# Splitting the key and query products of a segment in two, in a newly planned order of instructions

## The chip, the core and the metric

The kernel runs on one core of a Trainium2 chip. The metric is device microseconds (us) of one execution; the kernel before took 809.02 us (median of three runs, 808.73 to 811.75). Names of engines: PE multiplies matrices (PEld is its weight load, which overlaps PE), DVE and ACT are the vector and the scalar engine, POOL is GpSimd, SP issues the transfers (DMA).

## What is computed

Two attention layers read the same 2048 x 512 input `x`, and a gate mixes their outputs. Everything is bf16.

```python
g = sigmoid((x * gate_w).sum(-1, keepdims=True))
a = A(x, mem0, Wq, Wk, Wv, Wo)           # 32 heads of 128, 64 segments of 32 tokens
b = B(x, wq, wk, wv, wo, beta)           # 32 heads of 16, 4 stages of 512 tokens
return g * a + (1 - g) * b

# A: a recurrence. Each segment attends over 8 memory rows and its own 32 tokens,
# and the 8 memory rows of its output are the next segment's memory.
for s in range(64):
    h = concat([mem, x[32 * s:32 * s + 32]])                # 40 x 512
    q, k, v = h @ Wq, h @ Wk, h @ Wv                        # 512 -> 32 heads x 128
    p = softmax(mask(q @ k.T / sqrt(128)))
    o = (p @ v) @ Wo                                        # back to 512
    mem, out[s] = o[:8], o[8:]
# B: per stage a causal softmax over 512 tokens, plus a linear-attention memory
# of the stages before, mixed by sigmoid(beta) per head; then @ wo.
```

So A is 64 steps, each of which needs the output product of the one before; B has no such chain, except a small sum from stage to stage.

## The kernel before, in words

**Tiling.** In a segment of A only 32 rows (24 tokens and the 8 memory rows) are multiplied when the segment comes; the other 8 tokens of each segment don't depend on the memory in their projections and are done for four segments at once, ahead of time ("rest" work, `p_rest`: `rq`, `rk`, `rv`). With 32 rows as the stationary side, PE is split into four column tiles of 32, so that four products run side by side: a projection of 512 features onto half of the heads (`r` = 0 or 1) is 4 chunks `c` of the 512 features times 4 tiles, 16 matmuls of 512 columns. `wproj` writes it. A segment `s` (`p_seg`) is, by the names used below:

- `k0`, `q0`, `k1`, `q1`: key and query products of the two halves of the heads (tile `pb<-Wk_sb,hT`, `pb<-Wq_sb,hT`; line 1466 for products with a weight load, line 124 where the weights already in PE are used again). `q1` is done as two pieces of 256 columns. Each is evicted from PSUM (line 1040) and transposed by DVE (line 1544).
- `v0`, `v1`: value products (`pb<-Wv_sb,hT`), each in four pieces of one chunk, with other work allowed between the pieces.
- `H`, `S`: mask and scores (lines 1067 and 1559, 1563); `exp` on ACT (1568).
- `U`: the softmax sums by a product with ones (1586 and 124); ACT makes the reciprocals as exp(-ln) (1589, 1591), DVE multiplies them in (1593; the part of the rest rows in 1595, on DVE or POOL).
- `PV`, `PW`: probabilities times own values and times rest values (1626, 1635), evicted by ACT and DVE (1040).
- `wo`: the output product, 8 pieces of 8 matmuls of 256 columns (1352). DVE transposes the sum (1370), two small copies swap its halves (1374, each on ACT or DVE), and an addition writes the memory columns of the next segment's `hT` (1377). The first projection of the next segment waits for that.

B's work (`b...`: logits `bL` line 1184, their exps 1202, masks on POOL 1208, values `bPV` 1225, projections `bk`, `bq`, `bV`, rows `brow`), the rest work and its output product `wor` are put between the steps of A, to cover A's waits.

**Rest values.** `rv` of four segments is evicted into one of three staging tiles `stg` and stored to DRAM by four transfers (`rvst`, line 1431, `rest_v<-stg`), from where later segments load it (`rem_v<-rest_v`). A staging tile goes around: the next work that is given the tile may not be evicted into it before all four stores have landed, and since PSUM banks of this kind of work are handed out whole, the product itself waits for that too.

**What sets the order.** Every step is recorded with what it reads and writes. The order of instructions on each of the five queues (PE, ACT, DVE, POOL, SP) is fixed: it is unpacked from the table `ORDER`, a packed list of numbers, made by a planner of which the class `Prog` has the constants. Some steps may go to one of two engines; which one is in the table too. The planner's model of time (costs of steps; `FETCH`, the least time from one packet of 256 PE instructions to the next; `load`, the time that a store occupies the path to memory) puts out no instruction. It set the order, and with the table given it still decides which of the eight PSUM banks a step gets, and which semaphore a step has to look at.

**Weights kept.** `Share` and `turn`: where two projections of a segment stand directly behind each other on PE, the second starts with the chunk whose 32 columns of `hT` are still loaded, and leaves that weight load out (line 124).

```python
            for _ in range(o.size):
                c = held[1] if held and held[0] == key and held[1] in left else left[0]
                o.plan.append((c, held != (key, c), len(left) == o.share.total, len(left) == 1))
```

Of the kernel before, what the change touches and what calls it, by code (L numbers as in the profile page):

```python
# [15 lines left out]
    "c-nPY2Vhji)1STeF4uA?v>=^?&|5%yhY+L$k)VQrAcWpkgiu0n(u)*9k<bOC_Z~XZi6|=kK|vr1sdu@%x9^*MS6(^31g`Acot^TV-^^~-M`r8XMp|Ig6oFooTVNYGXX@;)^wVtFn%O{L-i3n@*B#C`"  # L16
    "cT8)`LDw(V+82JAtt+I@qaW7dJ+F6O<rWX!RP=Jz<srAqWx$1DtA>?2_3if0W`@qlw5DbQY`7VjYwVpKQ)%I}LVoT<LJ8;GqD_E^HxQonL(&U?D!)}Z7!SLWTI$>Y`$7ugVO=9QjPTkF@LQGo06jhD"
    "&Q3Ym!9(@~!1dJ0nwXEtthlv}Yv|lJp+VC#zq_F3L-=~*fA|>6Xh}2vQj3=*&viP~>T>O<pIcsQ05@`Mjp1%BfO83ln}0VFZl8rF=_!Q(99wdt9qcs~m_GUek_jPtx7o=#PoGH*b!d1EK+VT#Jz+=6"
    "%sy=PxfW~ztO2<4e)@5K?MQRBz1}H(c-0FQPazm_`ZIvaZa6aHwO=~g1P1FTL~G41=E~KYxJ&@EM+^5M&JDi;v?>5FdM6%*0+YQXuhp6z#<%u@Fjt-^a>GbBoc<ba0T{gV;LDw;Qpx5QU*TNdhC4y1"
    "tN9t6+H`(9H^jj_NR+m(p7wC5XFWhSo^uo5WIzSpz<bY1Km~Xnm<eTI;m)h59<L{8*i#(Hw_;S>`2btSFG@zwCG>thRTBM2_dVVBKy!Za1VSu0Y}Pq7kUQ!7{E_IQ<T({3)0(B=%euRwzF$s<5H2gE"  # L20
    "&;*OdgUJosf1fFt)((cPy4vtD3Cqztv=-g<xE!1dM(s6-Go5V$%bQ+=asK_MrlQ99Q|U3TCwg0ck=0pf*Fi3v=n;LlCcr%={xrl(;&%_hIKs`BBuxKW@7AFjXA<3c7Wlo~6M!0Sn9ss+O|lT-7XvrU"
    "e-kaQMGKq215}3K15@$}82&mE)=J*{14=b4Lj3$wt<YNRaadM}1_hgpo1i;bVACg(5~~;DO9hW3kDyqa1I+oMPQ-Q>OCId&3C@gIC@u#@e*Fs(Q+Ykw##Df$W7(XDOtfvSy^kcee!poeC-QpqvC#pG"
    "rs^C}xCmf=E}Owg)2jZ-c7KUbCzf@+0qoAgABO<$y%NT-c^q^&hBF?;K*`GMT0M@-vY8z?)$yR(vl`jYAR54}Gr+BSTVgYkVa;c#=$au+ZaIJ)Tj@+uf#$bd1WgFN6H^aiTkDU?4*^wyul>%NG#kD#"
    "o^1)R6Ya{zIOm`q4#&}MnmV_bU58-xF-haQ%`UV!2OXKlm>JW)h7d!xiD_)`>We=u&qA?R#Ts10k5<$mG|wwC8}sKkh(U?Fa>p)C4#Wy|g_wRD`YvYLipb3mojvZ`3Fy?RFd1USXa@FQ3k|Mq7#P=`"
    "C6M0u!7ki66oC%y(&znh78YIm_lg99Ut#hr_!v<@Y*Fw}6uf?8%{3K_TbpNb+4Egy*m{1egsu-^?!?cd+v^>AKC?;@v^&{$U%1=Tb{}HlTHZr+95}`fhL#c-j$s<)W$Yw`<8o}dwgRv>ypV6yusoWs"
    "`w}+&H$~EVJUHN|f!h#b=#94f?L`G)PLgNIv+?Fa-T<!TCGei4O5C=U(6CK|<88FzZyBZ3x?^`%hTFAYq8njv5^RS_|AWsq`^}6MU+oT}%`tOtN;}YTI`^kPYGDQ2*$wOTqb1pxRF#~w`G_3m>w_PF"
    "(Glttb7*a%9llSL(ZsRqaR8aq_=vnsy^FoJ^Lp;(xx`FU0Yo~?9w;<GKBF(6jR!gd4BrSkcPXt^^U{oT@mEQtplrsj%Nn<E!vZ)6kT6NkZ$7p#xg#?5T5$e2f)uVB6uMv}d0u)+3IkM{;Zwg0A5?=?"
# [126 lines left out]
class Slot(Res):  # L154
# [27 lines left out]
class Prog:  # L182
# [17 lines left out]
    FETCH = 3.55  # L200
# [1496 lines left out]
```

## Time and profile before

| | |
|---|---|
| runs | 808.73, 809.02, 811.75 us; median 809.02 |
| the profiled execution | 809.81 us, of which the span of instructions is 808.1 us |
| clock granted to PE | 1.000 over the span |
| PE busy | 788.1 us (98%), 23542 matmuls; 21898 weight loads |
| DVE, ACT, POOL busy | 609.9 us (75%), 560.4 us (69%), 249.1 us (31%) |
| moved by DMA | 45.02 MB, of it 2.92 MB in 178 packets of instructions on one queue |

Rows of the profile give an engine, a line, the tiles (out<-in), the sizes and a count; a row of waits names who waited, for whom, the sum in us, how often, and the longest. Rows of the timeline start with the start in us and the length; what stands in brackets is how long the engine had been idle and what ended it. Four matmuls on four column tiles run at the same time, so a row of four of 512 columns, with 0.39 us, is not four times 0.39. PE counts as busy while any is under way.

### The profile page before, as it was taken

The numbers are of one execution on the slowest core, as the hardware profiler recorded it, in microseconds if no ns is written. First come the engines' busy times: TensorE is split into PE (matmuls) and PEld (weight loads), VectorE is DVE, ScalarE is ACT, GpSimd is POOL, SyncE is SP. The second block draws the span as 40 slices with busy tenths as digits, with TensorE's granted clock in tenths as the row PEclk, the third lists the DMA queues.
The fourth block names the chain that finished last, engine by engine and source line by source line (L and its number), as shares of the span: only waits on it lengthen the run. The fifth ranks groups of instructions, "written<-read, shape, count | busy, mean of one in ns | idle before, by whom it ended". The sixth has DMA issues, their size and how long they took to land.

```text
span 808.1 us, 50000 instructions
## 1 busy us (share of the span) xinstructions
PE 788.1 (98%) x23542; PEld 466.1 (58%) x21898; DVE 609.9 (75%) x1578; ACT 560.4 (69%) x1322; POOL 249.1 (31%) x543
## 2 busy tenths in 40 slices
PE   9989999999999999999999999999999999999997
PEld 4445656656565566555567565565655655556655
DVE  4868776878888777777666777788867788776876
ACT  3676676676766766767777687676677776767773
POOL 3533231232332323431323331433323313323340
PEclk9999999999999999999999999999999999999999
DMA  8992112211111210111011211111020100000011
GB/s 314 417 273 45 44 30 50 44 30 30 46 31 28 41 34 20 45 35 46 20 35 40 46 44 17 33 29 26 28 59 23 43 24 16 11 26 16 17 35 36
DMA packets 71689, 45.02 MB, mean 56 GB/s; under 512 B 50046, under 2 KB 69942, under 8 KB 69942
## 3 DMA queue, kind: packets, MB, share of 16 engines
q1 hardware_dynamic: 70422, 40.92, 18.1%
q8 instruction: 178, 2.92, 1.5%
q10 hardware_dynamic: 1056, 0.92, 0.4%
q14 instruction: 33, 0.27, 0.1%
HBM read 30.33 MB, written 8.87 MB: 49 GB/s over the span
## 4 chain that ended last, share of the span: by engine, by line
PE 88%; DVE 5%; ACT 3%; DMA 1%; issue 1%; POOL 1%; SPq 0%; DVEq 0%; POOLq 0%
PE pb L1466 42%; PE pb L1352 18%; PE pb L124 6%; PE pb L1067 6%; PE pb L1184 4%; PE pb L1069 3%; PE pb L1225 2%; PE pb L1626 2%; PE pb L1559 1%; DMA rest_v<-stg 1%; PE pb L1586 1%; PE pb L827 1%; PE pb L1635 1%; PE pb L1563 1%; PE pb L1273 1%
## 5 line engine op out<-in xcount | busy, mean ns | idle before, releaser
L1040 ACT ACTIVATE st<-pb 128x512 bf16<-128x512 f32 (+2 forms) x291 | 135.3, 489 | 78.7 <-PE pb L1466 68.6
L1202 ACT ACTIVATE PTB<-pb 128x640 bf16<-128x640 f32 x240 | 157.6, 706 | 27.2 <-PE pb L1184 25.1
L1466 PE MATMUL pb<-Wv_sb,hT 128*32 128x512 bf16 x1760 | 139.0, 380 | 0.0
L1352 PE MATMUL pb<-Wo_sb,OT_sb 128*32 128x256 bf16 x4096 | 134.2, 274 | 3.1 <-issue 1.9
L1466 PE MATMUL pb<-Wq_sb,hT 128*32 128x256 bf16 (+1 forms) x2604 | 129.8, 311 | 1.0 <-DVE hT L1377 0.6
L1466 PE MATMUL pb<-Wk_sb,hT 128*32 128x512 bf16 x1716 | 116.5, 379 | 0.2
L1352 PEld LDWEIGHTS pb<-Wo_sb,OT_sb 128*32 128x32 bf16 x4096 | 99.4, 96 | 19.5 <-ACT OT_sb L1040 2.8
L1208 POOL TENSOR_SCALAR_AFFINE_SELECT PTB<-PTB 128x512 bf16<-128x512 bf16 x120 | 78.0, 650 | 98.2 <-ACT PTB L1202 92.8
L1466 PEld LDWEIGHTS pb<-Wq_sb,hT 128*32 128x32 bf16 x2604 | 67.5, 97 | 58.1 <-issue 32.4
L1040 ACT ACTIVATE OT_sb<-pb 128x320 bf16<-128x320 f32 (+2 forms) x162 | 65.7, 426 | 46.2 <-PE pb L1635 45.5
L1466 PEld LDWEIGHTS pb<-Wk_sb,hT 128*32 128x32 bf16 x1716 | 45.8, 97 | 53.3 <-issue 17.5
L1544 DVE STREAM_TRANSPOSE QT_sb<-st 128x128 f32<-128x128 f32 (+1 forms) x192 | 62.5, 336 | 17.3 <-ACT st L1040 15.3
L1595 POOL TENSOR_TENSOR PT_sb<-PT_sb,rc_sb 128x64 bf16<-128x64 bf16 x68 | 25.8, 379 | 155.3 <-ACT rc_sb L1591 154.1
L1544 DVE STREAM_TRANSPOSE KT_sb<-st 128x256 f32<-128x256 f32 x128 | 55.3, 432 | 18.2 <-ACT st L1040 16.5
L1040 DVE CAST V_sb<-pb 128x512 bf16<-128x512 f32 x82 | 56.1, 685 | 14.9 <-PE pb L1466 14.0
L1589 ACT ACTIVATE rc_sb<-pb 128x160 f32<-128x160 f32 x128 | 38.8, 303 | 36.3 <-PE pb L124 36.0
L1370 DVE STREAM_TRANSPOSE pb<-pb 128x256 f32<-128x256 f32 x63 | 29.3, 465 | 44.8 <-PE pb L1352 44.4
L1040 DVE CAST OT_sb<-pb 128x320 bf16<-128x320 f32 x98 | 47.1, 481 | 19.2 <-PE pb L1635 18.3
L1466 PEld LDWEIGHTS pb<-Wv_sb,hT 128*32 128x32 bf16 x1760 | 43.6, 98 | 24.4 <-issue 4.3
L1517 POOL COPY QT_sb<-rem_q 128x256 bf16<-128x256 bf16 x64 | 28.9, 452 | 89.9 <-PE pb L1563 63.0
L1593 DVE TENSOR_TENSOR PT_sb<-PT_sb,rc_sb 128x160 bf16<-128x160 bf16 x128 | 43.8, 342 | 14.4 <-ACT rc_sb L1591 13.1
L1568 ACT ACTIVATE PT_sb<-pb 128x224 bf16<-128x224 f32 x128 | 45.3, 355 | 12.4 <-PE pb L1563 7.9
(211 smaller groups left out, 1576.6 us busy)
## 6 DMA issues: line engine op xcount, KB each, us to landing
Wv_sb<-in_A_Wv_dram SPq DMA_DIRECT2D x4, 1024.0 KB, 10.9
Wk_sb<-in_A_Wk_dram SPq DMA_DIRECT2D x4, 1024.0 KB, 20.3
Wq_sb<-in_A_Wq_dram SPq DMA_DIRECT2D x4, 1024.0 KB, 27.5
Wo_sb<-in_A_Wo_dram SPq DMA_DIRECT2D x4, 1024.0 KB, 21.1
rest_v<-stg SPq DMA_DIRECT2D x112, 32.0 KB
rem_v<-rest_v SPq DMA_DIRECT2D x28, 128.0 KB, 2.3
a_rows<-ao SPq DMA_DIRECT2D x63, 32.0 KB
stg<-a_rows SPq DMA_DIRECT2D x15, 128.0 KB
```

The lines of the kernel that those rows point to most:

```text
L124: return pe.add_instruction(mybir.InstMatmult(name=pe.bass.get_next_instruction_name(), start_tensor_calc=start, stop_tensor_calc=stop, in ...
L1040: self.P.op(("act", "dve"), (lambda a: a.activation(dst, src(), ACT.Copy), lambda d: d.tensor_copy(dst, src())), reads=reads, writes=write ...
L1067: ins = pe.matmul(out[32 * c:32 * c + 32], lhsT[:, 32 * c:32 * c + 32], rhs, start=start, stop=stop, tile_position=(0, 32 * c), **kw)
L1184: ins = pe.matmul(pb[slot.banks[i]][:, base + a - lo:base + b - lo], KT[r0:r1, 128 * kc:128 * kc + 128], Q[r0:r1, t0 + a:t0 + b], start=Tr ...
L1202: P.op("act", (lambda dst=dst, src=src: lambda a: a.activation(dst, src(), ACT.Exp, scale=0.25))(), reads=[pair], writes=["%s%d_%d" % (nam ...
L1208: P.op("gp", (lambda pt=pt, ii=ii: (lambda g: g.affine_select(pt, pt, ([[0, len(ii)]] if len(ii) > 1 else []) + [[1, 128]], ALU.is_ge, 0.0 ...
L1352: ins = pe.matmul(pb[so.b][p0:p0 + 32, 0:256], tok(r, g, l), half(h, d, q), start=(r == 0 and g == 0 and l < 2), stop=(r == 1 and g == 3 a ...
L1466: ins = pe.matmul(out, own, part[:, g], start=start, stop=stop, tile_position=(0, 32 * g))
L1544: op("dve", (lambda dst=dst, src=src: lambda d: d.transpose(dst, src))(), reads=["st%d%s" % (i, tag)], writes=["%sT%d%s" % (kind, r, tag)] ...
L1568: op("act", lambda a: a.activation(PT[:, r, :], pb[rb.b][:, 0:224], ACT.Exp, scale=SCALE), reads=[rb], writes=["PT%d" % r, "PT%dr" % r], n ...
L1589: op("act", lambda a: a.activation(rc[:, r, :], pb[rb.b][:, 0:160], ACT.Ln), reads=[rb], writes=[rr], name="ln%d_%d" % (s, r), cost=0.325, ...
L1593: op("dve", lambda d: d.tensor_tensor(mine[r], mine[r], by_head(rc[:, r, :]), ALU.mult), reads=[rp, rr], writes=[rp], name="nrm%d_%d" % (s ...
```

## The change

Four edits. The key and query products of segments 1 to 63 are recorded as two steps of two chunks instead of one of four (`n` from 1 to 2), so that other PE work can stand between the halves, and either half can begin with the chunk that is loaded; `q1`, already two pieces by columns, becomes four steps. Two of the planner's constants change: `FETCH` from 3.55 to 3.95, and the `load` of each of the four stores of rest values from 0.1 to 0.35. And `ORDER` is another table (three lines longer, so that line 1466 before is line 1469 now, and so on), made with these.

```diff
 ORDER = (
-    "c-nPY2Vhji)1STeF4uA?v>=^?&|5%yhY+L$k)VQrAcWpkgiu0n(u)*9k<bOC_Z~XZi6|=kK|vr1sdu@%x9^*MS6(^31g`Acot^TV-^^~-M`r8XMp|Ig6oFooTVNYGXX@;)^wVtFn%O{L-i3n@*B#C`"
+    "c-nPY2VfM{*8XO;mt@oEAwdvB=p|HXN{3Jtq&)-_LJ8Fe0s=}$Q3N4Cq)3x49qCB#JOrf|6%YYKLJGS{cK6PIW@dM1W;cHzyV*OpobsLToOAbPIIk-({aY+6{G~158R^c87&7w<&#cd96!QFZaF{y*"
 ...
     BLOCK = 256
     BLOCK_AT = 190.0
-    FETCH = 3.55
+    FETCH = 3.95
 ...
                     P.dma(group, lambda s, l=l: s.dma_start(dst[:, :, l, r, :], st[:, 128 * l:128 * l + 128]), reads=[rs], writes=["dv%d_%d_%d" % (j, r, l)],
-                          name="rvst%d_%d_%d" % (j, r, l), prio=prio + 0.001 * l, load=0.1, cost=0.4)
+                          name="rvst%d_%d_%d" % (j, r, l), prio=prio + 0.001 * l, load=0.35, cost=0.4)
 ...
                 self.wproj(rb, kind, r, hv, [rx, rm], "%s%d_%d%s" % (kind, s, r, tag), prio, 4 if kind == "v" or s == 0 else 1,
+                self.wproj(rb, kind, r, hv, [rx, rm], "%s%d_%d%s" % (kind, s, r, tag), prio, 4 if kind == "v" or s == 0 else 2,
                            ("own", s) if s else None, lo, hi)
```

What the new table does on the queues is seen at three places. In the rows of the order, a line, the operation, out<-in, the size of the output, and how many of them follow each other.

**Transfers around the stores of rest values `rv8_0`** (SP). `rest_v<-stg` are the stores of the staging tile, `a_rows<-ao` are rows of finished segments, `DMA_TRANSPOSE xT` fetches input of a later stage. Before:

```order
L1316 DMA stg<-a_rows 128x512
L1487 DMA rem_v<-rest_v 128x512
L1431 DMA rest_v<-stg 4x32x128 x3
L947 DMA_TRANSPOSE xT<-in_A_x_dram 128x4x128
L1662 DMA a_rows<-ao 2x32x256 x2
L1431 DMA rest_v<-stg 4x32x128
L1329 DMA out_dram<-stg 128x512
```

and now:

```order
L1319 DMA stg<-a_rows 128x512
L950 DMA_TRANSPOSE xT<-in_A_x_dram 128x4x128
L1026 DMA wvB_sb<-in_B_wv_dram 128x4x128
L1026 DMA wqB_sb<-in_B_wq_dram 128x4x128
L1434 DMA rest_v<-stg 4x32x128 x3
L1665 DMA a_rows<-ao 2x32x256
L1434 DMA rest_v<-stg 4x32x128
L1332 DMA out_dram<-stg 128x512
```

The fourth store stood behind three other transfers, one of them a transposing one; now it stands behind one.

**From the output product of segment 52 to the first projection of segment 53** (PE). Before:

```order
L1352 MATMUL pb<-Wo_sb,OT_sb 32x256 x56
L1067 MATMUL pb<-hide_sb,neg_sb 32x4x40 x4
L1466 MATMUL pb<-Wk_sb,xr 32x512 x4
L1184 MATMUL pb<-QTm,KT_1 128x320 x4
L1466 MATMUL pb<-Wk_sb,xr 32x512 x4
L1466 MATMUL pb<-Wq_sb,hT 32x512 x16
```

and now:

```order
L1355 MATMUL pb<-Wo_sb,OT_sb 32x256 x64
L1187 MATMUL pb<-QTm,KT_1 128x320 x4
L1469 MATMUL pb<-Wk_sb,hT 32x512 x8
L127 MATMUL pb<-Wq_sb,hT 32x512 x4
L1469 MATMUL pb<-Wq_sb,hT 32x512 x12
```

Four groups of other work stood between the two; now one does, the piece of B's logits. Here the first half of the key product (8 matmuls) is followed by the whole query product, which begins with the loaded chunk.

**From the sums of segment 42 to its probabilities times values** (PE; the first row is the last product with ones, `Wv_sb,hT` are value products of the segment). Before:

```order
L124 MATMUL pb<-PT_sb,ones_sb 32x4x16 x4
L1466 MATMUL pb<-Wv_sb,hT 32x512 x12
L1626 MATMUL pb<-PT_sb,V_sb 128x40 x16
L1635 MATMUL pb<-PT_sb,rem_v 128x4x16 x4
L1184 MATMUL pb<-QTm,KT_1 128x64 x4
L1184 MATMUL pb<-QTm,KT_1 128x256 x4
L1626 MATMUL pb<-PT_sb,V_sb 128x40 x16
```

and now:

```order
L127 MATMUL pb<-PT_sb,ones_sb 32x4x16 x4
L1469 MATMUL pb<-Wv_sb,hT 32x512 x4
L1629 MATMUL pb<-PT_sb,V_sb 128x40 x16
L1638 MATMUL pb<-PT_sb,rem_v 128x4x16 x4
L1187 MATMUL pb<-QTm,KT_1 128x64 x4
L1187 MATMUL pb<-QTm,KT_1 128x256 x4
L1629 MATMUL pb<-PT_sb,V_sb 128x40 x16
```

Eight of the twelve value products have been moved to earlier places of the segment.

Counted over the whole program: 23551 matmuls (23542 before) and 21642 weight loads (21898 before); the weights in PE are used again in 350 groups of four matmuls (283 before). PE changes from one tiling of its array to another 390 times in both. Of the 320 split products, 199 have both halves directly behind each other. 367 transfers on SP in both. DVE has 24 steps fewer (1554 for 1578), ACT 13 more, POOL 11 more.

More of the change, by code (lines that the diff above doesn't have):

```diff
@@ L20 @@
[L20 to L27, printed above, removed]
@@ new lines @@
+    "?Ot5M%u|hV*wlGvzswbb+|hZjpH$RcuU`1?mJ9gdwJvqV!<qS}vqQ3OpBk2ynRYZGJbU<z`C}X(ef>$|z+o}&K4;#l0DSrR<cVOMDSy4LT}+l6i2An2KS09mguU|)W9$1|bDd{br(G~#X#|%UE&#7e"
+    "U+M#NXY6<@Z-M?mtIaoRqstClf-woWc4qU53#g^LSqOclTg9J$Hj`GA)p1SWhUw_LPh!Jzj-b`aT4f)dX?dp6c{Fuh$ckuk<s!yq151W38HG!pHh2w~aiC4Zv%nTwKX853-v)bhraT7<-4<tfMs&uB"
+    "V@vezT)SJped@H{D`wxq>gu=q0Vc>lgOFW+9@_1~qS4UXbM2X}uD&RhLA&a5-S%7uvP!$LyKaIru%huu7*olzdXLrglIOy5^mte+>tP~C&y3(nkXDjV($5~ew#GLGSM0@<8O5?tz(r&o?5(HmEzaa)"
+    "uqFLs#KEbzl+EAh37l!P*D2aSmk*2C<?41qp9!0%`AHma=SI@Z&t`U4=HENF1iY7Vt9oSOU>lN(<Kc0T?Kh_6ivn5W?xTFBPo7O5kb!|Jzl$HOPMGt-Wk!a(%=$a!b-I^UT{gm&1F3GTemzk+qs}gL"
@@ new lines @@
+    "--0B3F$txgi$}ojoG{0(&wowkf^{@77vrauRFvLJziAIh1wE$Df;|&P>+8r&SiL+JjIz!ehjr)HE8D-1?jN`M74DK*QBU+%<k^hbUjBA9$I1He+^h=gAvD8M;8f#O#c5>``<UKrc_x(JUM&hvj`#A-"
+    "&YEkI^&JVgDyjaTmAH;NqEqCbjUxuo>n>4#7u-=fuxFG&HVO6^6?C|TT5imz2~*d+A2{gUxW9ndtDff`m<q||Ufy0CCqZk>(h=ilViM4~ks?`(HE`5ydcsQDlXX!d`*saO{57jF6LwqP0Xn`@dlW~O"
+    "B2{_m)#d?jLO$<}%8JQ;TID59G&S@4(9X7{3tU!&A&($~pSsc1fA_UNKU2g9O((nNn_6vkyowYt0=NEb3pW-Y{zb9w#^K*iB|p5TUp*oVIoc;;%xvd$U{Q`Jgh`Ralz0=U@Z6*G=m|u6*!AD{pxOCO"
+    "8`8(*rDM1_+4QW0JiBC7&kyzP*Y)W1E<G%NWY=>QczFXHSAa^QZLZgMW1DEc{)#a1Kz4YArzE@;wk&#k9uHGK8eP>_xy%FA@4Yz^gRziij-@rTC(5hlU}tBiWdmZK+VX6oQ62hhSWM&te&ffvB!0K?"
@@ new lines @@
+    "XsoDlA4!+cRKltFZ~9!202X7G74}?NVZX0ps{Tf=4hg8@R2xOl@3DB4K;E+1&sWCQ-q_$Bu9m;@4NTkIf0oapB{E<)yb^7+a7@nf$$9fJ9+kwXRHRvqmN<kj%RI$^AM;Ee9bd4gU-D*Jk|iOi)oC{t"
+    "Ui|C25<It&vJ72C6Gc5GYUdp`8qCQf%vqc%>kNgq0uHXtBPHTX-XpGPi{&2=PHGG{0l@VtTK6nE@@_>Zl7U05PS7gr4J1mcU&g{+5|9qH64!l6arEf;V^TaOL(+eJKbZ8n7N=u=sy+9+5ox3GeeN_x"
+    "`w3!L_x}myZ=-Yu!ZXMKaW9>s1<hHaE;hy$z}q|jm`uu(X3^NEBN0v}p+I;pQB%S{M;nkI=#0Is?YWUaM%6nQ!Y@~xQppz&E}My>n<oy0>0v2b-iCd<^ZDf;!@3s##`Hj1)Qe9PD|bTg{CQ+ElFKcz"
+    "_)dyMMCQN7==3ncIXP10_r1u9z$aucatJK>{G0!{$~|+I`(x#p{GDB3ce@ZZWgG;+031yAEwUO4ff~<g|1TG0@Q8dGol)|+@llPJpcVQhz?k`|=q$6J@1VH9;!x&^7+K(6m&hUhuxEkS!&tB~)oUcK"
@@ new lines @@
+    "`IJOE-vq1o@0U#WsI0hZa}v%qXia<|rWo)xNG8tbYT=6H#WsK9sp6Cd`0qRr*BS~9dWu|QSRs+W$&}AiHk~zTf(-c1!#nu2xR<i5R2{g@E^|5HVL^0;K^OIsc+}?6k^kKIrAuJzMX4nvetKY&$mV4j"
+    "^kF$V^!{09a#))m!vDri>7+n+21wmA&!y?cJkfF42zN$gZSN(*WBJH)7lvYb+x;^Xzonw~eXJ9G7WI;gdg;i<)bHf%Xd|IC!Mbz)Ml_K)fPz)0GiT8QM<Gb=oxR)`0=Rxstn%LFug2lcdtv5W(cW%k"
+    "qL|$oMr5CVx3o;e$=Hq3?<gx)i`lzxoE!|aBqGa51ej@d-LCN~u~rj%t_iLoAK(L-i4UMPE%=!@k-V&j!&M;ivCb2vKl(0SiTU9;MqRg3sO)<&>$&LNvM;1_iUS44vScGOoO%Ov))ys~d^Cna#ccfU"
+    "(&n!&EvNA{{njAYK3qjq<mYn~tl>nz#GDd!W|pxyje6vojoUig@|G7Ehf?-37K~Sn`#HW_aDS6jsUYSh(HkZDwVjE1$k}V~AL~ES_!qd+L0PeHGWlk5a=Mg^-1INX8CK=2yaI{%!;K1L43tt_ULP2o"
@@ new lines @@
+    "Zhp#}^LP=g1izf9Y+5kzM;%pwk#4N%9H$sLZRxi60KxNIqFm824j;J10OM(e2?JGJux}($MxEb4ykaruMCOR3PofkU3nJXu*uJc)4*C`wZDz+SCueqXu(<V<R;(UVdcQUOsl;3FMjB4<Q^amT6{;kK"
+    "6=IRaWtd$txv=T(#NDzuE8FrORKnUsG*m2e?EUW}fIbqmMcFA;<iQWXY?N@5DLcOVoy>gAj*Dd?mA}AUaW?ObdHMD9Z0MvFUYnEPP2fg^B2bToSie;wVU<-@4J7U&*ww}pMbnri`JYPZhmwzF`kXAW"
+    "{-j;IY<q7z+0czPIInCw9b$_6NkTPMNSqkJ<Q+MF-B>z7**5|!dRi?3$HWw1RGJ$`4*`uRj7)6~xTW?)&#bfM#X3Q*2Je-YsMeQY?Nrap^DOimCH_$_1NVyK8A=!~S2J8DELTMoach>Sq-d*-r;}*1"
+    "ZxuzAXuY_f;9z;IHRB@C`rzh{j9W*wl6P?D?fUm};r*Vy#gf+|j&ZSL8JkNxm3Zd;#C^Kqd66~TwQj|-EGjpedNvIBn^n#^$2wyVYxzI+4(VnF$L!n8$)!Cudq!+lgzHXSxK|J1(DhKydgo3r!04!~"
@@ L75 @@
+    "3`OP"
 )
```

91 lines of the change are left out of this document (40 added, 51 removed).

## The prediction

> **What bounds the kernel now.** I read the page first: how full PE is, and what the chain that ended last is made of.
>
> ```profile
> span 808.1 us, 50000 instructions
> PE 788.1 (98%) x23542; PEld 466.1 (58%) x21898; DVE 609.9 (75%) x1578; ACT 560.4 (69%) x1322; POOL 249.1 (31%) x543
> ...
> PE 88%; DVE 5%; ACT 3%; DMA 1%; issue 1%; POOL 1%; SPq 0%; DVEq 0%; POOLq 0%
> ```
>
> PE is the bound from end to end, and the change leaves its products as they are. So the only thing to be won or lost is the time in which PE stands still, and the view by stretches says where that is:
>
> ```profile
> 0.00:60.00 60.00, 55.56 (x986) 27.29 (x978) 38.18 (x101) 34.32 (x69) 26.45 (x72) 1.00 0.95 338
> ...
> 60.00:760.00 700.00, 690.75 (x21248) 413.42 (x19704) 536.35 (x1389) 499.51 (x1184) 209.92 (x447) 1.00 0.14 33
> ...
> 760.00:808.00 48.00, 41.78 (x1320) 25.41 (x1216) 35.36 (x90) 26.53 (x72) 12.76 (x26) 1.00 0.11 31
> ```
>
> The first column behind the length is PE's busy time: 4.4 us idle at the start, 9.3 us in the 700 us of steady work, 6.2 us at the end, at a granted clock of 1.00. Some 20 us in all is what an order can touch; 0.5% of the time, about what a measurement of this kernel can tell from no change, is 4.0 us of it. The waits of PE and of its weight load say on whom:
>
> ```profile
> PE pb L1352 <- issue: 2.3, 3, 1.4
> PE pb L1466 <- DMA rest_v<-stg: 1.3, 2, 0.9
> ...
> PE pb L1067 <- issue: 1.0, 3, 0.4
> ```
>
> ```profile
> PEld pb L1466 <- issue: 57.0, 179, 0.8
> ...
> PEld pb L1626 <- DVE PT_sb L1593: 10.0, 28, 0.7
> ...
> PEld pb L1466 <- DVE hT L1377: 6.7, 22, 0.6
> ```
>
> (Us in total, times, longest.) The 57.0 us is no loss: the weight loader idles while PE streams. What counts is the hand-over of the memory (`hT`), the probabilities (`PT_sb`), one store, and a few pauses with no releaser (`issue`).
>
> **The change, part by part.**
>
> *Halves.* The same 16 matmuls per product. Four side by side follow each other at 0.22 and 0.21 us, whether with a weight load or, as in the second row, without:
>
> ```profile
> 375.26 0.39 PE L1466 MATMUL pb<-Wv_sb,hT 128*32 128x512 bf16 x4
> ...
> 375.48 0.39 PE L124 MATMUL pb<-Wv_sb,hT 128*32 128x512 bf16 x4
> ...
> 375.69 0.39 PE L1466 MATMUL pb<-Wv_sb,hT 128*32 128x512 bf16 x4
> ```
>
> One load has this row on the page (mean 97 ns behind the busy time):
>
> ```profile
> L1466 PEld LDWEIGHTS pb<-Wq_sb,hT 128*32 128x32 bf16 x2604 | 67.5, 97 | 58.1 <-issue 32.4
> ```
>
> So the 256 weight loads that are left out (64 groups of four) save nothing on PE: cost 0, hidden under the streaming of the group before; if that cover were gone, 256 x 0.097 us / 4 side by side = 6 us would be at stake. The other bound is a penalty at the new seams; the value products, in single chunks already, show none (0.22, 0.21). Changes of tiling are 390 in both orders. I take 0.
>
> *The store.* The fourth store of `rv8_0`:
>
> ```profile
> 375.46 0.53 SPq L1431 DMA_DIRECT2D rest_v<-stg  x1
> ...
> 376.94 0.40 PE L124 MATMUL pb<-Wv_sb,hT 128*32 128x512 bf16 x4
> ...
> 378.22 0.40 PE L1466 MATMUL pb<-Wk_sb,xr 128*32 128x512 bf16 x4 [0.89 <-DMA rest_v<-stg]
> ```
>
> The value product issued at 376.94 needs 0.22 us; PE could go on at 377.16 and goes on at 378.22, 2.76 us after the store's issue: 1.06 us lost. Now one transfer instead of three stands between the third and fourth store, and the transposing one has been moved ahead of all four. Bounds: 0 (the transfers ahead of the four hold them all back) to -1.06; with 6.3 us of PE work between `rv8_0` and `rk8_0` (6.5 before) and the short queue, I take -1.06. The trace names no other late store, and the other covers are 5 us and up (4.6 us sufficed before). The Trainium skill ("DMA: Bandwidth & Descriptors", on where the 2 us go) puts a store's fixed cost at about 2 us, most of it the write receipt; by that PE would have lost about 0.3 us here, and the term would be -0.3.
>
> *Longer spacing of instruction packets.* The constant issues nothing. What it is meant for looks like this (weight loads in the middle of one run of products, which no other engine releases):
>
> ```profile
> 253.58 0.12 PEld L1352 LDWEIGHTS pb<-Wo_sb,OTr_sb 128*32 128x32 bf16 x7 [0.64 <-issue]
> ...
> 394.44 0.83 PE L1352 MATMUL pb<-Wo_sb,OT_sb 128*32 128x256 bf16 x22 [0.51 <-issue]
> ```
>
> I gave each group on PE its spacing from the rows and cut the order at every 256 PE instructions. Packets that hold under 3.95 us of work: 69 before, 62 now; under 3.55 us: 26 and 31. So the new order isn't thinner where it was dense. Bounds: -3.3 us (the 2.3 and 1.0 of PE's waits for issue all gone) to +3.3; I take 0, as the counts point both ways. The Trainium skill ("Runtime: NRT & Kernel Launch", on instruction fetch) says that crossing a block of 256 instructions is mostly hidden, which would make this term 0 whatever the order; the two pauses above speak against "hidden".
>
> *The new order.* Here is the hand-over from segment 52 to 53 before:
>
> ```profile
> 678.49 0.24 PE L1067 MATMUL pb<-hide_sb,neg_sb 128*32 128x160 bf16 x4
> ...
> 678.56 0.39 PE L1466 MATMUL pb<-Wk_sb,xr 128*32 128x512 bf16 x4
> ...
> 678.72 0.47 DVE L1370 STREAM_TRANSPOSE pb<-pb 128x256 f32<-128x256 f32 x1 [0.26 <-PE pb L1352]
> 679.00 0.10 PEld L1184 LDWEIGHTS pb<-QTm,KT 32*128 32x128 bf16 x4 [0.41 <-ACT PTB L1202]
> 679.01 0.31 PE L1184 MATMUL pb<-QTm,KT 32*128 32x320 bf16 x4
> 679.22 0.19 ACT L1374 ACTIVATE other_sb<-pb 64x32 f32<-64x32 f32 x1 [0.26 <-DVE pb L1370]
> ...
> 679.25 0.40 PE L1466 MATMUL pb<-Wk_sb,xr 128*32 128x512 bf16 x4
> 679.51 0.19 DVE L1377 TENSOR_TENSOR hT<-pb,other_sb 128x32 bf16<-128x32 f32 x1
> 679.75 0.55 PEld L1466 LDWEIGHTS pb<-Wq_sb,hT 128*32 128x32 bf16 x16 [0.40 <-DVE hT L1377]
> 679.76 1.05 PE L1466 MATMUL pb<-Wq_sb,hT 128*32 128x512 bf16 x16
> ```
>
> Transposition, two copies side by side and the addition need 1.27 us from the first matmul after the output product (678.49) to the first projection (679.76). PE's work in it was 0.07 + 0.22 + 0.24 + 0.22 and 0.11 at the change of tiling, 0.86: 0.4 us short. Now only the logits are left, 0.35 us: 0.9 us short. Done so for the hand-overs of segments 3 to 62 (0.16 us more where both copies are on one engine), the work falls short by 3.8 us in 20 of them before and by 5.3 us in 22 now: +1.5 us. Nothing stands in PE's queue that could fill it, so I take it whole.
>
> The same tally for the two other chains. From the sums to the probabilities times values, whose links are
>
> ```profile
> L1040 ACT ACTIVATE OT_sb<-pb 128x320 bf16<-128x320 f32 (+2 forms) x162 | 65.7, 426 | 46.2 <-PE pb L1635 45.5
> ...
> L1589 ACT ACTIVATE rc_sb<-pb 128x160 f32<-128x160 f32 x128 | 38.8, 303 | 36.3 <-PE pb L124 36.0
> ...
> L1593 DVE TENSOR_TENSOR PT_sb<-PT_sb,rc_sb 128x160 bf16<-128x160 bf16 x128 | 43.8, 342 | 14.4 <-ACT rc_sb L1591 13.1
> ```
>
> (two ACT steps of 0.3, one of DVE of 0.34, and the hops: 1.5 us), the shortfall goes from 2.95 to 4.05 us, in segment 42 because 8 matmuls, 0.43 us, left it. From there to the output product (an eviction of 0.43 and 0.3 of hops, as between the output product and its transposition) it goes from 1.75 to 3.3. Together +2.65. These waits take each other's place, as segment 61 shows, where the tally before has 0.9 us in front of the second `PV` and 0.54 in front of `wo`:
>
> ```profile
> 776.54 0.27 PE L1626 MATMUL pb<-PT_sb,V_sb 32*128 32x40 bf16 x16
> ...
> 777.25 1.17 PE L1352 MATMUL pb<-Wo_sb,OT_sb 128*32 128x256 bf16 x36 [0.34 <-DVE OT_sb L1040]
> ```
>
> The trace has 0 and 0.34. Bounds 0 and +2.65; I take half, +1.3. In front of the scores the tally goes from 4.8 to 8.25 in cases of some 0.15 us each, near its resolution, so I take 0 and keep +3.45 as an upper end. DVE gives 24 steps to ACT and POOL, which are at 69% and 31%, so I count nothing for it.
>
> *Sum.* -1.06 + 1.5 + 1.3 = +1.7 us on the profiled 809.8 us: 811.5. That execution lies 0.8 us over the median of the runs (809.0), so 810.7.
>
> **Rivals.**
> 1. *The thinner covers add up.* The mechanism is the wait between engines that the halving and the other order left with less work in it; it decides once half of the tally comes true beyond my sum. For it: every chain's shortfall grew. Against it: segment 61. With all of it, -1.06 + 1.5 + 2.65 + 3.45 = +6.5: 815.5 us, slower.
> 2. *The pauses of issue go.* The planner, told of a longer spacing, left little cover where it expected a pause, so waits and pauses fall together, and covers cost nothing: -1.06 - 3.3 = -4.4: 804.6 us, faster. For it: pauses such as that at 394.44 stood by themselves. Against it: the counts of dense packets. By the skill's page on the runtime this rival has nothing to win; as two rows show such pauses, I leave it its chance.
> 3. *It does nothing.* 199 of 320 pairs of halves stand directly together, the end of the kernel has nearly the same order, and PE's work is the same: 809.0 us, or 808.0 with the store.
>
> **How the numbers follow.** My forecast (0.40) and rival 3 (0.12) lie within 0.5% of 809.0 (805.0 to 813.1) but for a little on each side; rival 1 has 0.23, rival 2 0.25, a little more than the counts of packets give it, since the tally sees only what shrinks on PE's side. Faster 0.26, same 0.49, slower 0.25. As cases of both signs hold half the chance, the likeliest one's own range is 808 to 814. The range for all reaches to rival 2 with 3 us of PE's other idle time gone (801.6), and to rival 1 with a further 2.5 us of the 3.3 of pauses (818.0).
>
> **What would show it.** Right: PE's busy time in the middle still 98 to 99%; the row of `rest_v<-stg` gone from PE's waits; weight loads 21642, with more than 57 us of `issue` on the loader and no time for it; the waits for `hT` L1377 above 6.7 us and for `PT_sb` L1593 above 10.0. Wrong: PE's waits for issue at zero (rival 2), or waits in front of the scores, L1559, grown by more than 2 us (rival 1); a store or a load of rest values late at another segment; a queue on ACT or POOL, with their added steps, that holds up the exps; or a start, before 60 us, that ends at another time, which I took as equal because its transfers bound it.

## The result and the profile after

The changed kernel took 816.13 us (median of 6 runs, 813.7 to 816.81) beside 809.13 us before; ratio 1.0073, 95% interval 1.0053 to 1.0094: slower by 0.7%, some 6 us. I had put 810.7 us and "no change" first; what came is the time of rival 1. It lies outside the 808 to 814 us that I gave my own case, and inside the range for all cases. The profiled execution took 816.68 us. Its page:

```profile
span 814.9 us, 49775 instructions
PE 791.4 (97%) x23551; PEld 453.3 (56%) x21642; DVE 597.8 (73%) x1554; ACT 566.9 (70%) x1335; POOL 254.7 (31%) x554
...
PE 88%; DVE 5%; DMA 3%; ACT 2%; issue 1%; SPq 0%; POOL 0%; DVEq 0%; ACTq 0%; POOLq 0%
```

PE is the bound as before, and DMA has gone from 1% to 3% of the chain that ended last. By stretches (length, then PE's busy time):

```profile
0.00:60.00 60.00, 54.76 (x987) 26.80 (x975) 40.25 (x105) 34.26 (x66) 28.45 (x76) 1.00 0.95 335
60.00:760.00 700.00, 688.22 (x21065) 398.25 (x19289) 517.13 (x1351) 501.44 (x1187) 210.11 (x446) 1.00 0.15 33
760.00:815.00 55.00, 48.38 (x1512) 28.26 (x1384) 40.38 (x99) 31.24 (x82) 16.13 (x34) 0.99 0.11 31
```

PE stands still 5.2 us at the start (4.4 before) and 11.8 us in the 700 us of steady work (9.3 before), and the work left for the third stretch is 6.6 us more. The waits of PE itself, then of its weight load:

```profile
PE pb L1355 <- issue: 2.2, 4, 1.3
PE pb L1469 <- issue: 1.8, 2, 1.4
PE pb L1469 <- DVE hT L1380: 1.6, 5, 0.5
...
PE pb L1469 <- DMA rest_v<-stg: 1.0, 2, 0.8
...
PE pb L1469 <- DMA out_dram<-stg: 0.4, 1, 0.4
```

```profile
PEld pb L1469 <- issue: 69.1, 211, 1.7
...
PEld pb L1469 <- DVE hT L1380: 11.1, 32, 0.7
...
PEld pb L1629 <- DVE PT_sb L1596: 9.4, 26, 0.7
...
PEld pb L1355 <- ACT OT_sb L1043: 5.1, 13, 0.7
...
PEld pb L1355 <- DVE OT_sb L1043: 3.7, 11, 0.6
```

Before, the two rows of `OT` in front of the output product read

```profile
PEld pb L1352 <- ACT OT_sb L1040: 2.8, 8, 0.6
...
PEld pb L1352 <- DVE OT_sb L1040: 2.4, 9, 0.5
```

So `hT` stands at 11.1 us (6.7 before), `OT` at 8.8 (5.2), and the wait for a store of rest values is still there. These rows overlap with work of PE. So I took PE's lost time from the trace: for every two pieces of work that follow each other, the time from the first matmul to the next piece's, less the streaming time and less the median for that pair of kinds. Gaps above 0.06 us go to the operation that ended last before them; where all had long ended they are pauses without a releaser. In us, behind 55 us, one profiled execution each:

| execution | `hT` | `PT` | `OT` | other engines | stores, output | pauses | sum |
|---|---|---|---|---|---|---|---|
| before | 1.9 | 2.4 | 3.8 | 6.5 | 1.1 | 4.1 | 19.7 |
| after | 3.9 | 3.7 | 5.8 | 4.5 | 1.6 | 7.3 | 26.8 |

The sum is 7.1 us up, and the profiled executions are 6.9 us apart. So there are two candidates: the three hand-overs (+5.3, of which 2.0 come back at other engines) and the pauses (+3.2). The limit of 55 us flatters the kernel before, though. The 7.3 us after hold a pause of 1.6 us at 58 us; the 4.1 us before leave out its twin, which starts at 54 us and is the longest wait for `issue` in that kernel:

```profile
55.77 0.29 PE L1352 MATMUL pb<-Wo_sb,OT_sb 128*32 128x256 bf16 x3 [1.35 <-issue]
```

With it the pauses are some 5.5 us before and 7.3 after, +1.8.

**A slow chain.** Not every longer wait is a thinner cover. Segment 57 after:

```profile
737.63 0.34 ACT L1594 ACTIVATE rc_sb<-rc_sb 128x160 f32<-128x160 f32 x1
...
737.72 0.69 DVE L1043 CAST V_sb<-pb 128x512 bf16<-128x512 f32 x1
...
738.32 0.48 DVE L1043 CAST OT_sb<-pb 128x320 bf16<-128x320 f32 x1
...
738.81 0.63 POOL L1211 TENSOR_SCALAR_AFFINE_SELECT PTB<-PTB 128x512 bf16<-128x512 bf16 x1
...
738.84 0.78 DVE L1596 TENSOR_TENSOR PT_sb<-PT_sb,rc_sb 128x160 bf16<-128x160 bf16 x1
...
739.68 0.27 PE L1629 MATMUL pb<-PT_sb,V_sb 32*128 32x40 bf16 x16 [0.50 <-DVE PT_sb L1596]
```

The reciprocal sums are there at 737.97. DVE, with a value eviction and an `OT` eviction ahead of it in its queue, multiplies them in at 738.84, in 0.78 us instead of 0.34: PE waits 0.50 us for a chain that is slow.

The 0.78 us are POOL's doing. The mask on POOL (738.81 to 739.44) was under way when the multiplication started, and the multiplication ended 0.18 us after it. In the twelve executions with the true multiplication there are 44 that start with a mask under way and over 0.15 us of it left: every one ends 0.17 to 0.18 us after the mask, while the median of all is 0.32 us long. So DVE is held until POOL is done. Counted the same way, multiplications that ran longer than they do alone make up some 0.9 us of PE's wait for `PT` before and 2.4 us after, more than the whole growth of that wait.

I split each wait at the latency that the quickest tenth of such chains needs (1.48 us for `hT`, 0.77 for `OT`, 1.65 and 1.83 for the two parts of `PT`): what the chain takes beyond it is slowness, the rest is missing cover. This split is an estimate; no run takes the slow chains back by themselves.

| us, before to after | missing cover | slow chain |
|---|---|---|
| `hT` | 1.3 to 2.8 | 0.6 to 1.1 |
| `OT` | 2.0 to 3.0 | 1.8 to 2.7 |
| `PT` | 0.2 to 0.5 | 2.1 to 3.2 |
| sum | 3.5 to 6.3 | 4.6 to 7.1 |

**A pause.** At the end of the start, after:

```profile
58.16 0.39 PE L1469 MATMUL pb<-Wq_sb,xr 128*32 128x512 bf16 x2
60.00 0.39 PE L1469 MATMUL pb<-Wq_sb,xr 128*32 128x512 bf16 x2 [1.45 <-issue]
```

and the DMA from 55 to 61 us (queue, packets, MB, share of the engines):

```profile
q1 hardware_dynamic: 2360, 0.64, 88.4%
q8 instruction: 1, 0.02, 2.7%
```

Queue 8 brings PE's instructions, 256 in a packet (177 packets of 16 KB for 45193 matmuls and weight loads). This packet started at 55.90 and took 2.6 us, where the median is 1.1, among data transfers that kept 88% of the engines busy; it landed at 58.50, and PE went on 1.5 us later. Of the 13 pauses above 0.24 us behind 55 us in the two executions, 12 ended 1.2 to 1.7 us after a packet had landed. So did the one that starts at 54 us in the kernel before (1.4 us). A packet lands every 4.6 us, so chance would put one or two of the 13 there. The packets are what PE waits for.

### The profile page after: what moved, and what is told of

Read it like the earlier page. It is cut to its first block, busy times and chain, and to the rows that moved or that the text cites. A ratio compares the mean times of both kernels' runs of the same rounds, so it can differ in the third digit from the quotient of the medians.

```text
span 814.9 us, 49775 instructions
## 1 busy us (share of the span) xinstructions
PE 791.4 (97%) x23551; PEld 453.3 (56%) x21642; DVE 597.8 (73%) x1554; ACT 566.9 (70%) x1335; POOL 254.7 (31%) x554
## 4 chain that ended last, share of the span: by engine, by line
PE 88%; DVE 5%; DMA 3%; ACT 2%; issue 1%; SPq 0%; POOL 0%; DVEq 0%; ACTq 0%; POOLq 0%
PE pb L1469 41%; PE pb L1355 18%; PE pb L127 8%; PE pb L1070 6%; PE pb L1187 3%; PE pb L1072 2%; PE pb L1228 2%; PE pb L1629 2%; PE pb L1562 1%; DMA rest_v<-stg 1%; DVE V_sb L1043 1%; PE pb L1589 1%; DMA Wo_sb<-in_B_wq_dram 1%; PE pb L1638 1%; DVE OT_sb L1043 1%
## 5 line engine op out<-in xcount | busy, mean ns | idle before, releaser
L1043 ACT ACTIVATE st<-pb 128x512 bf16<-128x512 f32 (+2 forms) x297 | 141.0, 496 | 76.5 <-PE pb L1469 63.4
L1469 PE MATMUL pb<-Wq_sb,hT 128*32 128x256 bf16 (+1 forms) x2476 | 135.2, 313 | 1.1 <-DVE hT L1380 0.8
L1469 PE MATMUL pb<-Wv_sb,hT 128*32 128x512 bf16 x1688 | 134.3, 380 | 0.4 <-issue 0.4
L1469 PE MATMUL pb<-Wk_sb,hT 128*32 128x512 bf16 x1648 | 119.7, 379 | 0.9 <-DVE hT L1380 0.7
L1469 PEld LDWEIGHTS pb<-Wq_sb,hT 128*32 128x32 bf16 x2476 | 61.9, 97 | 65.1 <-issue 36.4
L1469 PEld LDWEIGHTS pb<-Wk_sb,hT 128*32 128x32 bf16 x1648 | 42.2, 97 | 51.6 <-issue 21.9
L1043 DVE CAST OT_sb<-pb 128x320 bf16<-128x320 f32 x99 | 47.3, 484 | 16.6 <-PE pb L1638 15.1
L1592 ACT ACTIVATE rc_sb<-pb 128x160 f32<-128x160 f32 x128 | 38.8, 303 | 27.6 <-PE pb L127 26.8
L1469 PEld LDWEIGHTS pb<-Wv_sb,hT 128*32 128x32 bf16 x1688 | 41.7, 98 | 25.2 <-issue 7.3
L1043 ACT ACTIVATE stg<-pb 128x512 bf16<-128x512 f32 (+1 forms) x73 | 40.6, 559 | 13.6 <-PE pb L1469 9.8
```

Of the source, the lines that this page charges most:

```text
L1043: self.P.op(("act", "dve"), (lambda a: a.activation(dst, src(), ACT.Copy), lambda d: d.tensor_copy(dst, src())), reads=reads, writes=write ...
L1469: ins = pe.matmul(out, own, part[:, g], start=start, stop=stop, tile_position=(0, 32 * g))
L1592: op("act", lambda a: a.activation(rc[:, r, :], pb[rb.b][:, 0:160], ACT.Ln), reads=[rb], writes=[rr], name="ln%d_%d" % (s, r), cost=0.325, ...
```

## The experiments

Theory A: the order loses the time, in the hand-overs. Theory B: the halves do. Theory C: the pauses do, and follow from where packets end. Theory D, the reason for which I had halved two chains: waits take each other's place. Times of before beside the runs were 808.8 to 809.4 us. The constants need no run: the kernel after with `FETCH` 3.55 and `load` 0.1 has the same instructions in the same PSUM banks on all five queues, since the table fixes the order; two waits in front of one matmul change places, and nothing else does.

**The halves alone.** The edit, `n` and a re-encoded table:

```diff
-  ... "%s%d_%d%s" % (kind, s, r, tag), prio, 4 if kind == "v" or s == 0 else 1,
+  ... "%s%d_%d%s" % (kind, s, r, tag), prio, 4 if kind == "v" or s == 0 else 2,
-  PE: ... k5_0 ...          (order of before)
+  PE: ... k5_0 k5_0_2 ...
```

> The order before, word for word, with each key and query product cut into its two halves, which stay directly behind each other; nothing else differs. Theory A (the loss is in the order: less PE work inside the hand-overs, and instruction packets that come later): 809 us as before, within 1.5 us, PE's waits as before. Theory B (cutting the products costs time by itself, at 315 seams): some 7 us more, 816. Theory C (the pauses in front of late instruction packets are a matter of where the packets' ends fall): 809, since no instruction is added or removed on PE but weight loads that the two halves share.

809.91 us, 1.0008 (0.9995 to 1.0021). PE's busy time is that of before, with no seam in it:

```profile
span 806.6 us, 50000 instructions
PE 789.0 (98%) x23542; PEld 463.9 (58%) x21898; DVE 610.1 (76%) x1578; ACT 560.6 (70%) x1322; POOL 248.9 (31%) x543
```

B falls. (The seams are those of segments 1 to 63, five products in each; the 320 split products counted further up take in five of segment 0, which had been in pieces before. So 116 of 315 pairs stand apart in the new order.) The run shares no more weights than the kernel before (21898 loads), so it says nothing of the loads left out.

**The halves put together in the new order.** The reverse edit, with `k5_0_2` taken out of the table of after wherever it stood, and the PSUM banks kept as they were.

> The order after, with each second half put directly behind its first half again and both issued as one product; what stood between them comes behind. Theory A: 816, or a little more where the halves were apart (120 of 315), since the order is the new one otherwise: 814 to 818. Theory B: the 7 us come back, 809 to 811. Theory C: about 816, moved by up to 2 us either way as the weight loads change the packets' ends.

816.80 us, 1.0112 (1.0078 to 1.0146), with six runs from 814.5 to 823.4. Nothing comes back, and 264 weight loads more than in the kernel after (21906) make no difference that these runs can tell. Where the halves had stood apart, the second had been cover: waits before the scores go from 0.8 to 2.6 us and those for the exps from 0.2 to 1.7.

**Packets that end elsewhere**, twice in each order:

```diff
-  return pe.matmul(pb[sw.b][:, 0:512], phiK[:, 0, :], phiQ, start=True, stop=True)
+  ins = pe.matmul(pb[sw.b][:, 0:64], phiK[:, 0, :], phiQ[:, 0:64], start=True, stop=True)
+  for p in range(64, 512, 64):      # in 9, or 16 and 17, warm-up steps
+      ins = again(pe, pb[sw.b][:, p:p + 64], phiK[:, 0, :], phiQ[:, p:p + 64], True, True, (0, 128))
```

> The order before, with 112 more PE instructions in the first 6 us, where PE only warms up while it waits for the inputs: 16 warm-up products of 512 columns are cut into eight of 64. Every packet of 256 instructions thus ends at another place of the work. Theory A: the pauses without a releaser (4.1 us behind 55 us) stay within 1 us, since the order makes them; 809. Theory C: they change by 1 to 3 us and the time with them, 807 to 812.

> The order after, with 119 more PE instructions in the first 6 us, by cutting 17 warm-up products into eight. Theory A: the pauses without a releaser (7.3 us behind 55 us) stay within 1 us; 816. Theory C: the two long pauses of 1.6 and 1.4 us at 58 and 123 us go, and others come; pauses 3 to 6 us, time 812 to 815, and the waits on other engines stay 3 to 5 us above those before.

> The order before with 63 more PE instructions in the first 6 us, half as many as in the earlier shift. Theory C (pauses in front of packets follow from where the packets end): again another sum of pauses, between 2 and 7 us behind 55 us, and 808 to 812 us. If the order made them, 4 us as in the unshifted one, and 809.

> The order after with 63 more PE instructions in the first 6 us. Theory A with C: the waits for other engines stay at 3.5 to 4 us above those before wherever the packets end, the pauses come out between 3 and 7 us, and the time between 814 and 818 us, 5 to 7 us above the order before with its three placements on average.

| lost time behind 55 us | median, us | ratio (interval) | three hand-overs | pauses |
|---|---|---|---|---|
| before | 809.1 | | 8.0 | 4.1 |
| split_before | 809.9 | 1.0008 (0.9995 to 1.0021) | 8.3 | 2.2 |
| shift63_before | 810.5 | 1.0017 (1.0005 to 1.0029) | 8.0 | 4.4 |
| shift_before | 811.3 | 1.0026 (1.0011 to 1.0041) | 7.7 | 6.7 |
| after | 816.1 | 1.0073 (1.0053 to 1.0094) | 13.4 | 7.3 |
| shift63_after | 816.6 | 1.0097 (1.0078 to 1.0116) | 13.9 | 8.9 |
| shift_after | 815.9 | 1.0082 (1.0066 to 1.0097) | 13.2 | 6.7 |

The hand-overs belong to the order, to within 0.7 us, wherever the packets end. The pauses go from 2.2 to 6.7 us in one order, and up to 8.9 in the other (with the pauses that start at 54 us, before has 5.5 and split_before 3.0); moving the ends alone cost the order before 2 us. In the order after the numbers of C did not come: it had 3 to 6 us and 812 to 815 for the first shift, and 6.7 and 815.9 came, for which A's 1 us would do; it had 3 to 7 for the second, and 8.9 came. Each sum of pauses is that of one execution, and executions of one kernel spread by 5 us (before, beside the last series: 806.3 to 811.6). C holds for the pauses of the order before; it does not hold for the whole difference.

**What a missing cover costs.** In the order before, fillers are moved behind the step whose wait they covered, for example

```diff
-  PE: wo23_7 ... wor5_3 wor5_4 wor5_5 q24_0 <next product> ...      (hand-over, 17 times)
+  PE: wo23_7 ... q24_0 <next product> wor5_3 wor5_4 wor5_5 ...
-  PE: PW50_0 ... rv14_0_1 rv14_0_2 rv14_0_3 wo50_0 wo50_1 ...       (output, 10 times)
+  PE: PW50_0 ... wo50_0 wo50_1 rv14_0_1 rv14_0_2 rv14_0_3 ...
```

> The order before, with the cover of 17 hand-overs of the memory thinned: two or three fillers (products of the rest rows or of the other branch) that stood between the output product and the next segment's first projection now stand behind that projection's second product. By the tally, which needs 1.33 us of work there, this leaves them 0.35 to 0.6 us short, 8.3 us in all (none was short before). Theory A (a missing cover is lost in full): 817 us, with the wait for hT up by 7 to 9 us. Theory D (waits take each other's place, later covers grow by what was moved): 4 us or less come of it, 811 to 813.

826.25 us, 1.0209 (1.0188 to 1.0229): 17 us, twice the tally and more than either theory had. Waits of PE and of its weight load:

```profile
PE pb L1479 <- DVE hT L1390: 5.9, 17, 0.6
PE pb L1479 <- DVE stg L1340: 2.5, 3, 1.1
```

```profile
PEld pb L1479 <- DVE hT L1390: 17.2, 37, 0.9
```

Lost for `hT`: 8.4 us instead of 1.9, or 6.5 of the 8.3 that the tally names. The rest lies where the moved fillers were themselves awaited: lost time for other engines goes from 6.5 to 16.6 us, the row of `stg` among it.

> The order before, with the cover between the last product of probabilities and values and the output product thinned in 10 segments: fillers are moved behind the output product's second piece. By the tally, which needs 0.75 us there, this leaves 0.42 to 0.58 us short each, 4.5 us in all. Theory A: 813.5 us, wait for OT up by 4 to 5 us. Theory D, by which my prediction halved this chain: 2.2 us or less, 811.5.

817.63 us, 1.0106 (1.0089 to 1.0123).

```profile
PE pb L1365 <- ACT OT_sb L1053: 2.2, 7, 0.5
PE pb L1365 <- DVE OT_sb L1053: 2.1, 6, 0.6
```

Lost for `OT`: 7.8 us instead of 3.8, so 4.0 of the 4.5 of the tally; pauses, stores and other engines make up as much again. D fails in this direction: no other wait shrank in exchange.

**Two chains shortened.** The output differs, as the expectation says.

```diff
-  hm:  tensor_tensor(mem, turned, other, ADD)       after both swap copies
+  hm:  tensor_tensor(mem, turned, constant, ADD)    ahead of them
-  nrm, nrr:  tensor_tensor(PT, PT, rc, MULT)
+  nrm, nrr:  tensor_tensor(PT, PT, constant, MULT)
```

> The order before with two of the chains shortened, and every operation still issued: the addition that writes the memory's hT takes a constant instead of the swapped copy, and stands ahead of the copies (chain shorter by some 0.25 us); the probabilities are multiplied by a constant instead of the reciprocal sums (U to PV shorter by the two ACT steps, 0.9 us). The output is thus another one. Waits before: 1.9 us for hT, 2.4 for the probabilities, 3.8 for OT. Theory A: the first falls to about 0.5, the second to 0, nothing replaces them: 805.5 us. Theory D: half or more comes back in front of the output product, 807.5 or more.

> The same shortening of two chains in the order after. Waits there: 3.9 us for hT, 3.7 for the probabilities, 5.8 for OT. Theory A: the first falls to about 1.2, the second to 0: 809.7 us, so that the new order is 4.3 us above the old one instead of 7. Theory D: 3 us or less are won, 813 or more. Theory C (the difference is late instruction packets): both orders win alike, and 6 to 7 us stay between them.

810.51 us, 1.0014 (1.0000 to 1.0029), and 812.63 us, 1.0041 (1.0023 to 1.0059). What PE loses for `hT` goes from 1.9 to 0 and from 3.9 to 0.5 us. `PT` hardly moves in the order before (2.4 to 2.6): DVE gets to the multiplication only behind what stands ahead of it in its queue, and POOL holds it for longer (1.4 us of the wait instead of 0.9). After, it goes from 3.7 to 2.5. In neither order does it fall to 0, as Theory A had it. Between the orders 2.1 us stay of 7. That fits the chains, of whose difference 2.9 us are gone; but the pauses of the profiled executions, 9.2 and 10.2 us, now differ by 1.0 us instead of 3.2, so these runs alone do not show that the chains are most of it. The order before won nothing: its other engines' waits rose from 6.5 to 9.3 us, after from 4.5 to 8.6. That is D, in the direction of gains. A wait that goes is followed by the next one; a cover that goes is paid almost in full (6.5 of 8.3 us, 4.0 of 4.5).

**The store.** One edit on SP each:

```diff
-  SP: rvst8_0_0 rvst8_0_3 rvst8_0_2 dma_x3_2 ast26 ast25 rvst8_0_1      (before)
+  SP: rvst8_0_0 rvst8_0_3 rvst8_0_2 rvst8_0_1 dma_x3_2 ast26 ast25
-  SP: rvst5_0_0 dma_wvB7 rvst5_0_2 ast13 rlv14 rvst5_0_1 rvst5_0_3      (after)
+  SP: rvst5_0_0 rvst5_0_2 rvst5_0_1 rvst5_0_3 rlv14 dma_wvB7 ast13
```

> The order before with one edit on SP: the fourth store of rv8_0 is issued directly behind the other three, ahead of the transposing load and the two stores of rows that stood between. It is the term of my sum for the store, by itself. If the term is right, PE's wait for the store in front of rk8_0 (1.06 us lost) goes and nothing comes back: 808 us, too little for the runs to tell, so the trace has to show it. Rival: the next store that lands late holds PE at another place, as in the order after: the row for rest_v<-stg stays at 1 us or so.

> The order after with one edit on SP: the four stores of rv5_0 are issued one behind the other, ahead of the load of rest values for segment 14, a weight load and a store of rows that stood between them. PE's wait in front of rk5_0 (1.03 us) goes if its place in SP's queue made it; 815 us. Rival: the load of rest values then comes too late for the second product of probabilities and values of segment 14, and the 1 us stays.

The wait after, which the second edit is about:

```profile
227.41 0.21 PE L127 MATMUL pb<-PT_sb,ones_sb 128*32 128x64 bf16 x4
228.46 0.40 PE L1469 MATMUL pb<-Wk_sb,xr 128*32 128x512 bf16 x4 [0.85 <-DMA rest_v<-stg]
```

with SP's queue ahead of it:

```profile
223.03 0.51 SPq L1434 DMA_DIRECT2D rest_v<-stg  x1
223.58 0.51 SPq L1665 DMA_DIRECT2D a_rows<-ao  x1
224.13 0.45 SPq L1490 DMA_DIRECT2D rem_v<-rest_v  x1
224.62 1.14 SPq L1434 DMA_DIRECT2D rest_v<-stg  x2
```

store_before: 808.23 us, 0.9991 (0.9977 to 1.0004), and these rows:

```profile
PE pb L1479 <- DMA rest_v<-stg: 0.3, 1, 0.3
PE pb L1479 <- DMA out_dram<-stg: 0.2, 1, 0.2
```

The wait at `rk8_0` is gone, and a wait of 0.35 us for a store of output at `rq7_0` is new. store_after: 812.66 us, 1.0049 (1.0029 to 1.0070), where 815 had been expected.

```profile
PE pb L1482 <- DMA rest_v<-stg: 0.6, 1, 0.6
PE pb L1482 <- DMA out_dram<-stg: 0.5, 1, 0.5
```

The wait at `rk5_0` is gone; the lost time for stores and output is 0.8 us instead of 1.6. That explains 0.8 of the 3.5 us by which it beats the kernel after. The rest seems to be in the pauses (2.0 us in its profiled execution, 7.3 in that of after), though PE's instructions are the same one by one. The execution profiled was the fastest of nine, so its 2.0 us is a low figure. Why its packets come in time stays open.

The two repaired kernels compare the orders with the waits for these stores out of both: 4.4 us between the runs, and 4.6 us between their lost times without the pauses (14.6 and 19.2). So the hand-overs, less what comes back at other engines, are the greater part of the 7 us; the pauses and the store are the rest. None of the kernels measurably beats the one before.

## Where the prediction was right and where wrong

- **Halves, 0:** right. Cutting the products costs 0.08%, with an interval across 0, and leaves no seam in PE's busy time. That the loads left out save nothing agrees with merge_after, but its six runs are too far apart to show it well.
- **Store, -1.06:** wrong as a term, though the mechanism was right. Moving that store does remove the wait, as the edit by itself shows; but in the new table the stores of `rv5_0` stand in the same way behind a weight load, a store of rows and a load of rest values: 1.03 us at `rk5_0`, and 0.18 at `rk13_0`. I had looked at the place that the trace named and not at the other stores of the new order. Measured with the stores of output: +0.5.
- **Packets, 0:** +3.2 us behind 55 us between the profiled executions, or +1.8 with the pause at 54 us before. My counts of dense packets (69 to 62, 26 to 31) said nothing of it: the sums run from 2 to 9 us with the places where packets end, and differ even where these are the same. The bound of 3.3 held, and it belonged into the range of every case. The Trainium skill ("Runtime: NRT & Kernel Launch", on instruction fetch) calls the crossing mostly hidden. The trace after agrees so far as only eight pauses above 0.24 us go with its 177 packets; but these cost 0.3 to 1.6 us each, so the term is not 0.
- **Hand-over, +1.5:** the cover part is +1.5 by the split above, which is an estimate. The wait grew by 2.0, as the chains were also slower by 0.5.
- **The two other chains, +1.3 of a tally of 2.65:** missing cover +1.3 by the same estimate, but not for my reason, so the size is luck: thinning a cover costs 0.9 of the tally at the output and 0.8 at the hand-over, with nothing given back. The tally was too high for `PT` (1.1 against 0.3) and nearer for `OT` (1.55 against 1.0).
- **Steps from DVE to ACT and POOL, 0:** the reasoning failed most clearly. It counted the share of busy time of ACT and POOL; what counts is the place of each link in its queue, and what POOL is at when DVE multiplies. Slow chains cost +2.5 us over the three hand-overs by the estimate above, and I had no term for them. That the steps that moved make them is not shown: in segment 57 the two evictions ahead of the multiplication are DVE's own in both orders, and that of `OT` stood behind it before. For `PT` it is the hold by POOL that grew, by 1.5 us.
- **Scores, 0:** right, 0.9 and 0.8 us. **Other engines**, for which I had no term, gave 2.0 back. **The start, 0:** PE stands still 0.8 us more in the first 60 us, in which each kernel has one long pause.

Together: 2.8 (cover) + 2.5 (slow chains) + 1.6 (pauses behind 60 us) + 0.8 (the first 60 us) + 0.5 (stores) - 2.0 (other engines) = +6.2 of +6.9 us; the rest is not accounted for, gaps below 0.06 us among it. Rival 1 had the right time by partly wrong terms, which is luck: it counted 3.45 us in front of the scores, which did not come, and neither pauses nor queues. Of what I said would show it, the weight loads (21642, 69.1 us of `issue`) and `hT` above 6.7 came true; `PT_sb` went to 9.4 instead of above 10.0, and the store's row stayed. Of the signs of being wrong, a late store at another segment came, and not the waits in front of the scores.

## What to carry to other kernels

When an order is replaced, price each wait twice: the work of the waiting engine that covers it, and the queue positions of every link of the chain it waits for. A cover taken away cost 0.8 to 0.9 of its shortfall here, and as much again or more where the moved work was itself awaited, while a chain made shorter pays only as far as the next wait. Look, too, at what POOL does while DVE multiplies. After a late transfer is cured, list all its kin in the new order, and keep the pauses for instruction packets in the range, since moving the ends of the packets alone shifted this kernel by 2 us.

## What had not been expected of the hardware

PE resumes 1.2 to 1.7 us after a late packet of instructions has landed, however short the transfer (1.1 us in the median, 2.6 us among the data transfers at 56 us). The sum of these pauses differs by 5 us between one execution each of two kernels whose PE instructions are identical (2.0 and 7.3 us). A multiplication on DVE that starts while POOL is at a mask ends 0.17 to 0.18 us after the mask, in all 44 cases with over 0.15 us of the mask left: 0.78 instead of 0.34 us in segment 57.
